# One chip program, re-ordered: an RWKV6 scan feeding a leaky-ReLU MLP, with the same steps in a new order and with other engine choices

## The chip, the cores and the metric

One core of a Trainium2 chip. Its engines are TensorE (PE: matmuls; PEld: its weight loads), VectorE (DVE), ScalarE (ACT), GpSimd (POOL) and SyncE (SP), which here issues nearly all DMAs. Each engine runs its own instructions in program order and waits on semaphores for the others. The metric is device time in microseconds of one execution, and the times given are medians over runs.

## The reference

Inputs r, k, v, w are (4 batches, 8 heads, 768 positions, 48), u is (8, 48). A recurrence with a 48 x 48 state for each head runs over the positions; its output, 3072 rows of 384, goes through a two-layer MLP (384 to 2048 to 384).

```python
for t in range(S):
    cur = einsum('bhd,bhe->bhde', u[None] * kt, vt)
    y[:, :, t] = einsum('bhd,bhde->bhe', rt, state + cur)
    state = wt[:, :, :, None] * state + einsum('bhd,bhe->bhde', kt, vt)
x = y.transpose(0, 2, 1, 3).reshape(B * S, H * D)
h = x @ w_in
g = maximum(0.01 * h, h)
out = g @ w_out
```

All is float32 outside; the kernel multiplies in bfloat16.

## The kernel before

**Tiling.** The positions are cut into 24 chunks of 128 (6 for each batch). Chunks 0 to 3 come as two pairs: the first 256 positions of batch 0 and of batch 1, loaded as 384 KB transfers. The other 20 chunks are singles with four loads of 192 KB each (w, k, r, v; L708), all on SyncE's queue. `seq` interleaves the batches, so that neighbouring chunks belong to different recurrences.

**One chunk** (`single`). ACT takes the logarithm of w (L718), PE sums it along the chunk with a triangular matrix (L724), DVE forms the other sum (`ci`, L736), ACT takes two exponentials (L750, L754), and DVE multiplies r and k by them (`rk`, through `mult`, L407). The transposes of r and k go through PE and an evacuation (L418; L423 on DVE or L425 on ACT) or, for the chunks in `RK_DMA` (among them 16 to 23), through a DMA transpose issued by SyncE (L771). PE makes the scores (L864), DVE masks them (two instructions, L795), PE multiplies the state (L831) and the masked scores (L836) with the inputs, and DVE adds the bonus term and writes y (L482). The bonus comes from POOL (L437, L441), a DVE reduction (L445) and POOL again (`vs`, L449). POOL also casts v (L457) and scales the state (L782). y is transposed into the columns of x by PE (L468) and a copy, or by a DMA transpose (L849; chunks 16, 17, 20 to 23).

**MLP.** The chunks are grouped into 14 blocks (`blocks`: 0 and 5 to 13 have two chunks, 1 to 4 one). A block's up products (L1030) fill a PSUM bank eight times (four times for one chunk), and ACT applies the leaky ReLU to each (L1045). The first seven blocks use plain down products (L1060) and one output copy for each chunk (L1071 on DVE, L1073 on ACT). The last seven (`seven`) use a seven-product scheme for 2 x 2 blocks of the down matrix: DVE forms four sums of the activations (L941) and, once, four of the weights (L910), PE makes the products (L960), and ACT and DVE combine them (L976, L974, L981). The weights come as float32 on the same SyncE queue: four loads of 384 KB and two of 768 KB of w_in (L318), four of 768 KB of w_out (L323); each is cast to bfloat16 by POOL, ACT or DVE (L340, L344, L342).

**The order.** Nothing is scheduled on the chip. The functions above only register steps with `Plan.add`: the engines that could do it, with an estimated duration each, what it depends on, and which tile slots it reads and takes. `Plan.order` then walks the list `ORDER` (1124 step numbers), gives each step its engine (`FORCE` where there is a choice), computes estimated start times from the durations, chooses for each buffer the slot that is free first by those times, and the instructions are emitted in that order. So `ORDER` fixes the instruction stream of each engine and the order of SyncE's queue, and a step that waits holds everything behind it on its engine. Ahead of the first up products the kernel fills PE's estimated gaps up to 24 us with matmuls on zeros (L1099).

The heart of it, shortened:

```python
for i in ORDER:
    e = FORCE.get(i) or next(iter(engs))
    now = max(at[e], ready[i])
    for b in takes:
        slot = min(free[b.pool])
    self.start[i], self.eng[i] = now, e
...
for i in order:
    plan.steps[i][1](plan.eng[i])
```

Of the kernel before, what the change touches and what calls it, by code (L numbers as in the profile page):

```python
# [22 lines left out]
class Plan:  # L23
# [4 lines left out]
    SEEN = {"PE": 0.21, "DVE": 0.05, "ACT": 0.05, "POOL": 0.07, "SP": 0.05}  # L28

# [3 lines left out]
    def add(self, engs, fn, pri, deps=(), reads=(), takes=(), wire=None):  # L33
        i = len(self.steps)
        self.steps.append([engs, fn, pri, {d for d in deps if d is not None}, tuple(reads), tuple(takes), wire])
        for b in (*reads, *takes):
            b.users.append(i)
        return i

    def order(self, pools):  # L40
# [11 lines left out]
        at, wire_free, landed, flying = dict(self.BEGIN), 0.0, 0.0, []  # L52
        for i in ORDER:
            engs, fn, deps, reads, takes, wire = self.steps[i][0], *self.steps[i][1:2], *self.steps[i][3:]
# [10 lines left out]
            for b in touched:  # L65
                if b.pool == "ps":
                    now = max([now, *(t for q, t in b.seen.items() if q != e)])
            self.start[i], self.eng[i] = now, e
# [24 lines left out]
LOAD = (1.1, 64, 1.4, 0.2)  # L93
BOTH = (1.5, 64, 1.45, 0.2)
WEIGHT = (2.08, 24, 2.6, 0.2)
HALF = (1.1, 16, 2.6, 0.2)
STORE = (0.45, 8, 0.9, 0.2)
TRK = (1.7, 64, 0.9, -0.6)
TY = (0.95, 24, 0.7, -0.6)
ORDER = [1122, 0, 1, 2, 3, 4, 5, 6, 7, 11, 14, 20, 12, 18, 15, 17, 16, 13, 19, 21, 8, 22, 25, 26, 27, 23, 36,  # L100
# [67 lines left out]
def kernel(  # L168
# [11 lines left out]
    nc = tc.nc  # L180
# [79 lines left out]
    with tc.manual_schedule():  # L260
# [193 lines left out]
        def cast_v(P0, slots, vv, vl):  # L454
            vb = Buf("vb")
            return vb, step(
                {"POOL": 0.56}, lambda e: nc.gpsimd.tensor_copy(out=vb.t[:], in_=vv()),  # L457
                P0 + 2, deps=vl, reads=slots, takes=[vb])
# [675 lines left out]
```

## Time and profile before

| | us |
|---|---|
| median of 3 runs | 179.06 |
| lowest and highest run | 178.73, 179.62 |
| profiled execution, first to last instruction | 177.0 |
| PE busy in it | 170.4 |
| DVE busy in it | 143.5 |
| ACT busy in it | 114.0 |
| POOL busy in it | 107.3 |

The profiled execution is one run of the program under the profiler. Its span counts from its first to its last instruction; the times of the runs also hold what lies around the program, and the page gives no figure for that. In the profile's lines, "L960 PE" is line 960 of the kernel on TensorE, `out<-in` names the tiles, "x48" is a count, and "idle before <-X" is time in which the engine stood still until X was done. "SPq" is SyncE's queue. The granted TensorE clock was 1.00 throughout.

### The profile page before, as it was taken

Reading aid. Unit: us, or ns where it says so; the run is one execution under the profiler, and the core shown is the slowest. Engines: PE = TensorE matmul, PEld = TensorE weight load, DVE = VectorE, ACT = ScalarE, POOL = GpSimd, SP = SyncE. Lnnn points to the kernel's source line nnn. Section 1 sums busy time; section 2 is a strip of 40 time slices with the busy share of each in tenths; the row PEclk is TensorE's granted clock in tenths of the full one; section 3 lists DMA queues with packets and bytes.
Section 4 is the critical chain, followed back from the end, with each engine's and each line's share of the span. In section 5 each row is a group of like instructions: output and inputs, shape, how many; then the busy total and the mean of one; then the engine's idle time right before and its main releaser. Section 6 shows DMA issues by size and latency. Waiting matters only on the chain.

```text
span 177.0 us, 5530 instructions
## 1 busy us (share of the span) xinstructions
PE 170.4 (96%) x2155; PEld 139.9 (79%) x2158; DVE 143.5 (81%) x299; ACT 114.0 (64%) x263; POOL 107.3 (61%) x143
## 2 busy tenths in 40 slices
PE   7999999999999999999999999999999998999993
PEld 2566779867768877777779899899899997799992
DVE  7498935267599899889879999999999999956662
ACT  5676769734677794796379964676769950178500
POOL 5989946486749859879599093391693959100000
PEclk9999999999999999999999999999999999999999
DMA  5999999999999999999999999996999897432104
GB/s 138 261 271 340 350 300 195 351 231 199 201 206 195 191 199 227 163 201 179 198 206 195 197 208 209 163 222 124 210 194 196 188 226 78 118 101 80 44 26 157
DMA packets 115885, 34.25 MB, mean 194 GB/s; under 512 B 108305, under 2 KB 115090, under 8 KB 115858
## 3 DMA queue, kind: packets, MB, share of 16 engines
q1 hardware_dynamic: 115856, 33.89, 93.1%
q8 instruction: 17, 0.28, 0.7%
q14 instruction: 10, 0.08, 0.2%
q10 hardware_dynamic: 2, 0.00, 0.0%
HBM read 25.17 MB, written 4.72 MB: 169 GB/s over the span
## 4 chain that ended last, share of the span: by engine, by line
PE 69%; DVE 15%; ACT 5%; issue 4%; DMA 3%; POOL 2%; DVEq 0%; SPq 0%; ACTq 0%
PE ps L1030 30%; PE ps L1060 13%; PE ps L960 10%; DVE rk L407 3%; DMA rkT<-rk 3%; PE ps L864 3%; DVE in L941 2%; PE ps L418 2%; ACT g L425 2%; PE ps L724 1%; PE ps L836 1%; DVE ci L736 1%; PE ps L518 1%; DVE dg L445 1%; ACT ps L750 1%
## 5 line engine op out<-in xcount | busy, mean ns | idle before, releaser
L1030 PE MATMUL ps<-xT,w_in_b 128*128 128x256 bf16 (+1 forms) x672 | 70.8, 258 | 0.3 <-DVE rk L407 0.2
L1045 ACT ACTIVATE g<-ps 128x512 bf16<-128x512 f32 x96 | 54.4, 598 | 18.1 <-PE ps L1030 16.0
L1030 PEld LDWEIGHTS <-w_in_b 128*128 128x128 bf16 x672 | 56.9, 98 | 7.8 <-issue 0.6
L437 POOL TENSOR_TENSOR ru<-in,ub 128x384 f32<-128x384 f32 x24 | 24.3, 1017 | 13.1 <-DMA in<-in_k_dram 7.0
L1060 PE MATMUL ps<-w_out_b,g 128*128 128x384 bf16 x160 | 31.4, 326 | 0.0
L407 DVE TENSOR_TENSOR rk<-in,ps 128x384 bf16<-128x384 f32 x48 | 24.8, 547 | 6.1 <-ACT ps L754 2.3
L782 POOL TENSOR_TENSOR sb<-s,a 128x384 bf16<-128x384 f32 x18 | 15.6, 875 | 16.6 <-ACT a L745 8.1
L795 DVE TENSOR_TENSOR m<-ps,maskb 128x512 bf16<-128x512 f32 x40 | 25.1, 682 | 0.3 <-PE ps L864 0.2
L441 POOL TENSOR_TENSOR ru<-ru,in 128x384 f32<-128x384 f32 x24 | 23.8, 1000 | 2.1 <-DMA in<-in_r_dram 1.1
L1060 PEld LDWEIGHTS <-g 128*128 128x128 bf16 x160 | 14.1, 97 | 6.8
L449 POOL TENSOR_TENSOR vs<-in,dg 128x384 f32<-128x384 f32 x20 | 17.4, 874 | 3.0 <-DMA in<-in_v_dram 2.1
L960 PEld LDWEIGHTS <-g 128*128 128x128 bf16 x224 | 18.3, 98 | 0.2
L976 ACT COPY o<-ps 128x192 f32<-128x192 f32 x18 | 5.8, 320 | 17.5 <-PE ps L960 15.5
L960 PEld LDWEIGHTS <-in 128*128 128x128 bf16 x168 | 13.6, 98 | 1.9 <-DVE in L941 1.4
L445 DVE TENSOR_REDUCE dg<-ru 128x8 f32<-128x384 f32 x24 | 12.9, 545 | 1.9 <-POOL ru L441 1.7
L457 POOL CAST vb<-in 128x384 bf16<-128x384 f32 x24 | 12.7, 534 | 2.2 <-DMA in<-in_v_dram 2.2
L981 DVE TENSOR_TENSOR o<-ps,o 128x192 f32<-128x192 f32 x35 | 11.6, 351 | 1.9 <-ACT o L976 1.1
L482 DVE TENSOR_TENSOR y<-ps,vs 128x384 bf16<-128x384 f32 x20 | 10.9, 553 | 2.4 <-PE ps L836 2.3
L754 ACT ACTIVATE ps<-ci 128x384 f32<-128x384 f32 x20 | 9.8, 493 | 4.7 <-DVE ci L736 4.1
L718 ACT ACTIVATE lw<-in 128x384 bf16<-128x384 f32 x20 | 9.9, 521 | 4.1 <-DMA in<-in_w_dram 4.1
L736 DVE TENSOR_TENSOR ci<-ps,lw 128x384 f32<-128x384 f32 x20 | 10.9, 551 | 1.8 <-PE ps L724 1.1
L960 PE MATMUL ps<-in,in 128*128 128x192 bf16 x112 | 11.4, 247 | 0.5 <-DVE in L941 0.5
(105 smaller groups left out, 258.8 us busy)
## 6 DMA issues: line engine op xcount, KB each, us to landing
out_dram<-o SPq DMA_DIRECT2D x23, 192.0 KB, 2.8
in<-in_w_dram SPq DMA_DIRECT2D x20, 192.0 KB, 4.7
in<-in_k_dram SPq DMA_DIRECT2D x20, 192.0 KB, 4.2
in<-in_r_dram SPq DMA_DIRECT2D x20, 192.0 KB, 4.2
in<-in_v_dram SPq DMA_DIRECT2D x20, 192.0 KB, 4.1
in<-in_moe_w_out_dram SPq DMA_DIRECT2D x4, 768.0 KB, 6.9
in<-in_moe_w_in_dram SPq DMA_DIRECT2D x2, 768.0 KB, 9.7
in<-in_moe_w_in_dram SPq DMA_DIRECT2D x4, 384.0 KB, 8.1
```

Of the source, the lines that this page charges most:

```text
L407: (nc.gpsimd if e == "POOL" else nc.vector).tensor_tensor(out=o, in0=x, in1=i, op=ALU.mult)
L437: lambda e: nc.gpsimd.tensor_tensor(out=ru.t[:], in0=kv(), in1=ubv, op=ALU.mult),
L441: lambda e: nc.gpsimd.tensor_tensor(out=ru.t[:], in0=ru.t[:], in1=rv(), op=ALU.mult),
L445: lambda e: nc.vector.tensor_reduce(out=dg.t[:], in_=ru.t[:], axis=AX.X, op=ALU.add),
L449: lambda e: nc.gpsimd.tensor_tensor(out=vs.t[:], in0=vv(), in1=dg.t[:].unsqueeze(2).to_broadcast([128, H, D]), op=ALU.mult),
L457: {"POOL": 0.56}, lambda e: nc.gpsimd.tensor_copy(out=vb.t[:], in_=vv()),
L782: lambda e: nc.gpsimd.tensor_tensor(out=sb.t[:].rearrange("p g a d -> p (g a) d"), in0=s_in.t[:].rearrange("p g a d -> p (g a) d"), in1=a_ ...
L795: lambda e, par=par: nc.vector.tensor_tensor(out=m.t[:, par, :, :], in0=sc[par].t[:].rearrange("p (g t) -> p g t", g=NP), in1=maskb[:].uns ...
L960: nc.tensor.matmul(o(), lhsT=x()[:, i, :], rhs=y()[:, i, :], start=fresh, stop=(stop and i == ii[-1]), skip_group_check=True)
L1030: nc.tensor.matmul(hp.t[:, a * N : (a + 1) * N], lhsT=w_in_b[:, t, (j + a) * 128 : (j + a + 1) * 128], rhs=xb.t[:, t, 0:N], start=(a == 0 ...
L1045: lambda e, hp=hp, g=g, j=j, J=J, N=N: nc.scalar.activation(out=g.t[:, j : j + J, 0:N], in_=hp.t[:, 0 : J * N].rearrange("p (a n) -> p a n ...
L1060: nc.tensor.matmul(op.t[:, 0:DM], lhsT=g.t[:, j, off : off + 128], rhs=w_out_b[:, j, :], start=(j == 0), stop=(j == NJ - 1))
```

## The change

No operation of the computation changes. Four things do:

1. `ORDER` and `FORCE` are new lists. 45 of the steps with a choice of engine change it: 20 leave DVE and 20 come to it, and the totals go from 281, 262 and 125 steps on DVE, ACT and POOL to 281, 265 and 122.
2. The planner's estimates change: the durations of some steps, the times of the DMA transfers, and three new terms: steps marked `alone` on DVE and POOL steps are kept apart in the estimate, a limit on outstanding DMA descriptors (`RING`), and DMA time taken by PE's instruction fetches (`mm`, `FETCHED`). They reach the chip only through the slot chosen for each buffer and through the number of warm-up matmuls.
3. The steps' priorities (`pri`) get small additions; the emitted order does not read them.
4. All PE steps that were registered before it depend on the step that takes the warm-up bank.

What the new `ORDER` does, told by the steps: the second pair's v is loaded ahead of all weights (it stood behind a 768 KB and a 384 KB piece of w_in); chunk 4's loads of w, k and r come ahead of the last 768 KB of w_in, and of all of w_out; chunk 6's r comes ahead of its k and of the last piece of w_out. At the end, chunk 23's w and k are loaded ahead of chunk 22's, DVE multiplies r and k of chunk 23 ahead of those of 22, the transposes (L771) go out as 20, 21, 23, 22 with the v of chunk 22 between 21 and 23 and the v of chunk 23 and a store between 23 and 22; DVE's four sums (L941) of block 11 stand behind the y (L482) of chunks 23 and 22, and four product steps of that block stand on PE among the up products of the last two blocks.

The diff, without the bodies of the two lists:

```diff
@@ Plan
+    RING, AFTER, FETCH = 145.0, 0.25, 1.0
+    FETCHED = [120, 235, *(128 * n + 65 for n in range(2, 17))]
-    def add(self, engs, fn, pri, deps=(), reads=(), takes=(), wire=None):
+    def add(self, engs, fn, pri, deps=(), reads=(), takes=(), wire=None, alone=False, mm=0):
@@ Plan.order
+            if e == "POOL" or alone and e == "DVE":
+                mine, other = (spans[e], spans["DVE" if e == "POOL" else "POOL"])
+                for a, z in other:
+                    if a <= now < z:
+                        now = z
...
-                while flying and sum(x for _, x in flying) + size > 150:
-                    at[e] = max(at[e], flying.pop(0)[0])
-                wire_free = max(wire_free, at[e] + lead) + time
-                flying.append((wire_free, size))
-                landed = self.done[i] = max(wire_free + lat, landed + 0.7 * time)
+                held = now
+                while flying and sum(x for _, x in flying) + size > self.RING:
+                    held = max(held, flying.pop(0)[0])
+                at[e] = max(at[e], held + self.AFTER)
...
+                flying.append((max(wire_free, *late), size))
+                self.done[i] = flying[-1][0] + lat
@@ transfer estimates
-LOAD = (1.1, 64, 1.4, 0.2)
+LOAD = (1.012, 64, 1.72, 0.45)
...
-TRK = (1.7, 64, 0.9, -0.6)
+TRK = (1.368, 64, 1.24, 0.7)
@@ the lists (start and end of ORDER)
-ORDER = [1122, 0, 1, 2, 3, 4, 5, 6, 7, 11, 14, 20, 12, 18, 15, 17, 16, 13, 19, 21, 8, 22, 25, 26, 27, 23, 36,
...
-    1115, 1116, 1112, 1113, 1119, 1117, 1118, 1121]
+ORDER = [0, 1, 4, 2, 1122, 3, 5, 6, 7, 11, 12, 14, 13, 8, 18, 22, 20, 25, 9, 23, 26, 19, 63, 21, 28, 29, 15, 36, 27,
...
+    1115, 1116, 1112, 1113, 1117, 1118, 1119, 1121]
-FORCE = {4: "ACT", 6: "DVE", 24: "ACT", 27: "ACT", 30: "DVE", 33: "ACT", 47: "ACT", 57: "ACT", 59: "DVE", 60:
...
+FORCE = {4: "DVE", 6: "DVE", 24: "DVE", 27: "ACT", 30: "ACT", 33: "ACT", 47: "DVE", 57: "ACT", 59: "ACT", 60: "ACT",
...
@@ durations, one for many
-                {"PE": 0.19 + 0.231 * len(ns)}, scores, ns[-1] * 10 + 1, deps=[s for x in asked for s in x[2]],
+                {"PE": 0.12 + 0.221 * len(ns)}, scores, ns[-1] * 10 + 1, mm=H * len(ns), deps=[s for x in asked for s in x[2]],
@@ warm-up
-        step({"PE": 0.0}, lambda e: None, 0.0, takes=[warm])
+        warm_from = step({"PE": 0.0}, lambda e: None, 0.0, takes=[warm])
+        for i in range(warm_from):
+            if "PE" in plan.steps[i][0]:
+                plan.steps[i][3].add(warm_from)
```

More of the change, by code (lines that the diff above doesn't have):

```diff
@@ L51, in order @@
         self.start, self.done, self.eng, ready = [None] * n, [0.0] * n, [None] * n, [0.0] * n
-        at, wire_free, landed, flying = dict(self.BEGIN), 0.0, 0.0, []
+        at, wire_free, flying = dict(self.BEGIN), 0.0, []
+        late, fetches, products, block = [0.0, 0.0], [], 0, 0
+        spans = {"POOL": [], "DVE": []}
         for i in ORDER:
-            engs, fn, deps, reads, takes, wire = self.steps[i][0], *self.steps[i][1:2], *self.steps[i][3:]
+            engs, fn, deps, reads, takes, wire, alone, mm = self.steps[i][0], *self.steps[i][1:2], *self.steps[i][3:]
             if left[i]:
@@ L67, in order @@
                     now = max([now, *(t for q, t in b.seen.items() if q != e)])
+            if e == "POOL" or alone and e == "DVE":
[3 more added lines that the diff above has]
+                        now = z
+                for a, z in other:
+                    if now < a < now + engs[e]:
+                        at["DVE" if e == "POOL" else "POOL"] += now + engs[e] - a
+                        break
+                mine.append((now, now + engs[e]))
+                del mine[:-3]
             self.start[i], self.eng[i] = now, e
@@ L345, in weight_steps @@
                 (win_s if which == 0 else wout_s).append(step(
-                    {"DVE": 0.57, "ACT": 0.83, "POOL": 0.86 if which == 0 else 0.96}, cast, pri + 1, deps=[ld], reads=[st]))
+                    {"DVE": 0.57, "ACT": 0.83, "POOL": 0.83}, cast, pri + 1, deps=[ld], reads=[st], alone=True))
         xt_steps, lns, firsts, rows = {}, {}, {}, {}
@@ L520, in go @@
                                 start=(j == 0 and x.start == 0), stop=(j == 1), skip_group_check=True)
-                return step({"PE": 0.33}, go, P0, deps=[s_ln], reads=[lw], takes=[bank])
+                return step({"PE": 0.33}, go, P0, mm=2 * (len(parts) if split else 1), deps=[s_ln], reads=[lw], takes=[bank])
             c1, c0, cg, e0 = (Buf("ps", "cp2") for _ in range(4))
@@ L636, in scores @@
                                     start=True, stop=True, skip_group_check=True)
-                s_sc = step({"PE": 0.42}, scores, P0 + 1, deps=s_T, reads=[rkT], takes=sc)
+                s_sc = step({"PE": 0.35}, scores, P0 + 1, mm=4 * NP, deps=s_T, reads=[rkT], takes=sc)
                 m = Buf("m")
@@ L730, in cum @@
                         rhs=ones[:], start=True, stop=True, skip_group_check=True)
-            s_cum = firsts[n] = step({"PE": 0.27}, cum, P0, deps=[s_ln], reads=[lw], takes=[cp])
+            s_cum = firsts[n] = step({"PE": 0.27}, cum, P0, mm=1 if first else 1 + NP, deps=[s_ln], reads=[lw], takes=[cp])
             ci, ek = Buf("ci"), Buf("ps", "ek")
@@ L809, in sums @@
                             start=True, stop=True, skip_group_check=True)
-                s_pp = step({"PE": 0.17}, sums, P0 + 2, deps=[s_k, s_vb, s_sb], reads=[rk, vb], takes=[pp])
+                s_pp = step({"PE": 0.17}, sums, P0 + 2, mm=NP, deps=[s_k, s_vb, s_sb], reads=[rk, vb], takes=[pp])
                 def state(e):
@@ L911, in mix @@
                 last = done[x] = step(
-                    {"DVE": 0.95}, sub, MIX_RANK, deps=[*wout_s, last], reads=t[: x // 2 + 1], takes=[t[x // 2]])
+                    {"DVE": 0.95}, sub, MIX_RANK, deps=[*wout_s, last], reads=t[: x // 2 + 1], takes=[t[x // 2]], alone=True)
             mixed.extend([part, t, done])
@@ L943, in seven @@
                     before = step(
-                        {"DVE": 0.68} if len(groups) == 1 else {"DVE": 0.42}, go, SUM_RANK + x * 0.5, deps=[*deps, before],
-                        reads=[g], takes=[sm])
+                        {"DVE": 0.69} if len(groups) == 1 else {"DVE": 0.42}, go, SUM_RANK + x * 0.5 + nb / 64, deps=[*deps, before],
+                        reads=[g], takes=[sm], alone=True)
                     s_sum.setdefault(name, []).append(before)
@@ L976, in go @@
                         nc.scalar.copy(out=o(), in_=x())
-                return step({"ACT": 0.33, "DVE": 0.35}, go, 3, deps=deps, reads=reads, takes=[to])
+                return step({"ACT": 0.33, "DVE": 0.35}, go, 3 + nb / 64, deps=deps, reads=reads, takes=[to])
             def plus(to, o, x, y, deps, reads):
@@ L1073, in ocopy @@
                         nc.scalar.copy(out=o.t[:], in_=op.t[:, 0:DM])
-                s_o = step({"DVE": 0.55, "ACT": 0.5}, ocopy, 3, deps=[s_dn], reads=[op], takes=[o])
+                s_o = step({"DVE": 0.55, "ACT": 0.5}, ocopy, 3 + ch / 64, deps=[s_dn], reads=[op], takes=[o])
                 step(
```

78 lines of the change are left out of this document (44 added, 34 removed), and 100 rows, old and new, of the table ORDER.

## The prediction

> **What bounds the kernel now.** I read the page first, then the busy time by stretches, then the chain of waits in order of time, and last single stretches engine by engine. The page's span, its row of engines and the chain's shares:
>
> ```profile
> span 177.0 us, 5530 instructions
> ...
> PE 170.4 (96%) x2155; PEld 139.9 (79%) x2158; DVE 143.5 (81%) x299; ACT 114.0 (64%) x263; POOL 107.3 (61%) x143
> ...
> PE 69%; DVE 15%; ACT 5%; issue 4%; DMA 3%; POOL 2%; DVEq 0%; SPq 0%; ACTq 0%
> ```
>
> The same execution in five stretches. The columns are the stretch, its length, busy us (and instructions) of PE, PEld, DVE, ACT, POOL, then clock, DMA share and GB/s:
>
> ```profile
> 0.00:25.00 25.00, 22.71 (x312) 14.44 (x316) 18.95 (x49) 16.59 (x34) 20.98 (x39) 1.00 1.06 277
> 25.00:55.00 30.00, 29.69 (x366) 22.75 (x364) 18.94 (x39) 20.87 (x46) 18.85 (x23) 1.00 1.11 231
> 55.00:145.00 90.00, 89.94 (x1147) 77.12 (x1145) 83.35 (x162) 65.46 (x162) 61.50 (x75) 1.00 1.05 195
> 145.00:155.00 10.00, 9.04 (x130) 7.80 (x128) 9.68 (x18) 1.03 (x3) 5.93 (x8) 1.00 0.65 105
> 155.00:177.00 22.00, 19.01 (x211) 17.81 (x208) 12.61 (x33) 10.01 (x20) 0.00 (x0) 1.00 0.25 82
> ```
>
> PE looks full, but that is the pipeline: a busy PE may still leave slots. The pace of matmuls that follow each other without a gap stands in the chain in order of time (start, us, what):
>
> ```profile
> 31.37 0.65 PE ps L1060 x4
> 32.02 0.67 PE ps L1030 x12
> ...
> 52.31 0.55 PE ps L864 x16
> ...
> 56.82 0.20 PE ps L836 x8
> ...
> 155.59 7.21 PE ps L1030 x66
> ...
> 166.09 7.93 PE ps L960 x96
> ```
>
> So a down product (L1060) takes 0.65/4 = 0.1625 us, an up product (L1030) 0.67/12 = 0.056 us at 128 columns and 7.21/66 = 0.109 at 256, a last-block product (L960) 7.93/96 = 0.0826, a score (L864) 0.034, a masked product (L836) 0.025. From 155.59 to 174.0 (166.09 + 7.93) PE runs at this pace: that part is its own and cannot be shortened by an order. The matmuls are the same in both kernels, so only PE's lost slots ahead of 155 us can be won or added to. I look for them in two stretches. First 145 to 155 us, all of PE's matmul groups (count, then busy us and mean ns):
>
> ```profile
> L960 PE MATMUL ps<-in,g 128*128 128x192 bf16 x32 | 3.1, 246 | 0.0
> L960 PE MATMUL ps<-in,in 128*128 128x192 bf16 x18 | 2.0, 248 | 0.5 <-DVE in L941 0.5
> L960 PE MATMUL ps<-w_out_b,in 128*128 128x192 bf16 x16 | 1.7, 248 | 0.4 <-DVE in L941 0.4
> L1030 PE MATMUL ps<-xT,w_in_b 128*128 128x256 bf16 x12 | 1.5, 272 | 0.0
> L836 PE MATMUL ps<-vb,m 128*128 128x48 bf16 x24 | 1.1, 184 | 0.0
> L831 PE MATMUL ps<-sb,rkT 128*128 128x96 bf16 x12 | 1.0, 206 | 0.0
> L864 PE MATMUL ps<-rkT 48*128 48x128 bf16 x16 | 0.8, 218 | 0.0
> ```
>
> 66 x 0.0826 + 12 x 0.109 + 24 x 0.025 + 16 x 0.034 = 7.9 us, and about 0.5 for the twelve L831 (between 12 x 0.025 and 12 x 0.056): 8.4 of 10 us. **About 1.6 us are lost here**, and DVE, 9.68 of 10 busy, is what PE waits for. Second, 40 to 50 us:
>
> ```profile
> L1060 PE MATMUL ps<-w_out_b,g 128*128 128x384 bf16 x30 | 5.9, 327 | 0.0
> L1030 PE MATMUL ps<-xT,w_in_b 128*128 128x128 bf16 x48 | 3.2, 219 | 0.2 <-DVE rk L407 0.2
> L418 PE MATMUL ps<-ident,rk 128*128 128x128 bf16 x8 | 0.8, 221 | 0.1
> L724 PE MATMUL ps<-lw,trev 128*128 128x384 bf16 x2 | 0.7, 326 | 0.0
> L836 PE MATMUL ps<-vb,m 128*128 128x48 bf16 x8 | 0.5, 184 | 0.0
> ```
>
> 30 x 0.1625 + 48 x 0.056 + 8 x 0.056 + 2 x 0.1625 + 8 x 0.025 = 8.5, and some 0.6 for the 19 short ones left out (0.025 to 0.056 each): 9.1. **About 0.9 us are lost.** From 55 to 145 us I treat the losses as what an order of this kind costs, and move nothing there.
>
> The Trainium skill, page Perfetto Trace Analysis, section Identifying the Most-Contended Engine, would have PE judged by the busy share of its weight loads; by that 37 us (177.0 - 139.9) would be free. The rows disagree: four L1060 take 0.65 us with four loads of about 0.1 us beside them, so 0.25 us of "free" load time is no free PE; the sum goes by the paces.
>
> **The change, part by part.** What runs is altered in three ways: the order of 1124 steps, the engine of 45 of them, and the count of warm-up matmuls (L1099), which fill gaps that the plan expects in the first 24 us. The planner's other new terms only choose tile slots and those gaps.
>
> *Engines.* 20 steps leave DVE and 20 come to it (281 before and after), ACT goes from 262 to 265, POOL from 125 to 122. The largest one-way group is five output copies that go from DVE to ACT:
>
> ```profile
> L1071 DVE COPY o<-ps 128x384 f32<-128x384 f32 x5 | 2.8, 550 | 0.0
> ```
>
> DVE loses those 2.8 us and two state copies (as long as these), and takes two weight casts, a state copy and a few smaller copies more: about 1 us less over 150 us. On its own I cost this at nothing, since PE sets the pace.
>
> *Start, 0 to 25 us.* The second pair's v is loaded ahead of all of w_in instead of after two pieces of it. POOL's row for the casts of that v:
>
> ```profile
> 19.36 0.96 POOL L457 CAST vb<-in 128x384 bf16<-128x384 f32 x2 [0.43 <-DMA in<-in_v_dram]
> ```
>
> Gain at most that 0.43 wait and about half a us of casts taken off POOL ahead of it, so -1.0; against it w_in comes one 384 KB load later while the first columns of x are ready at about the same time, which at worst holds the first up products for a load's time, +1.0. I take -0.2, near zero as both chains end within that us.
>
> *25 to 55 us.* The lost 0.9 follows on late inputs: DVE waits for chunk 6's r, and SyncE held that load long before it:
>
> ```profile
> 45.47 0.55 DVE L407 TENSOR_TENSOR rk<-in,ps 128x384 bf16<-128x384 f32 x1 [1.22 <-DMA in<-in_r_dram]
> ```
> ```profile
> 38.34 4.28 SPq L708 DMA_DIRECT2D in<-in_r_dram  x1
> ```
>
> In the new order chunk 6's r stands ahead of its k and of the last 768 KB piece of w_out; it stood behind both. The wait of 1.22 should go; the bounds are 0 (something else is late next: ACT's exponentials, or w_out, whose pieces come later) and -0.9. I take -0.6.
>
> *145 to 155 us.* DVE's rows for the four sums (L941) of block 11 (chunks 18 and 19), 142.7 to 151.6:
>
> ```profile
> 142.72 0.68 DVE L941 TENSOR_TENSOR in<-g 128x1024 bf16<-128x1024 bf16 x1
> 143.44 0.69 DVE L941 TENSOR_TENSOR g<-g 128x1024 bf16<-128x1024 bf16 x1
> ...
> 149.02 1.30 DVE L941 TENSOR_TENSOR in<-in,g 128x1024 bf16<-128x1024 bf16 x1
> ...
> 150.51 1.04 DVE L941 TENSOR_TENSOR in<-g,in 128x1024 bf16<-128x1024 bf16 x1
> ```
>
> Two are stretched (1.30 and 1.04 against 0.68) while POOL works:
>
> ```profile
> 148.94 2.07 POOL L449 TENSOR_TENSOR vs<-in,dg 128x384 f32<-128x384 f32 x2
> ```
>
> The new order puts all four, and two additions (0.35 each), behind chunk 22's y (L482), after which POOL has nothing left to collide with. That takes 0.68 + 0.69 + 1.30 + 1.04 + 0.7 = 4.4 us from ahead of that y, less 0.55 for chunk 23's y, now ahead of it: 3.8. Where PE and DVE met before:
>
> ```profile
> 153.38 0.34 PE L831 MATMUL ps<-sb,rkT 128*128 128x96 bf16 x4
> ```
> ```profile
> 154.14 0.54 DVE L482 TENSOR_TENSOR y<-ps,vs 128x384 bf16<-128x384 f32 x1
> ```
>
> DVE could be at that y by 154.1 - 3.8 = 150.3. On PE, four product steps (32 x 0.0826 = 2.6 us) now stand behind chunk 22's L831 and chunk 23's (0.4) ahead, so without lost slots PE comes to it at 153.4 - 1.6 - 2.6 + 0.4 = 149.6. So the end moves by the new time of that L831, less 153.4, plus 2.2: at 149.6 all 1.6 us are won. DVE allows it, as its masks stand 2 us ahead of the y. What is late next is the transpose that feeds them. The two last transposes by SyncE, chunk 22's and then chunk 23's, and the page's row for all of them (KB, then median us to landing):
>
> ```profile
> 142.50 2.20 SPq L771 DMA_TRANSPOSE rkT<-rk  x1
> ...
> 147.51 1.24 SPq L771 DMA_TRANSPOSE rkT<-rk  x1
> ```
> ```profile
> rkT<-rk SPq DMA_TRANSPOSE x13, 3.8
> ```
>
> Their order is swapped: chunk 22's is now the last. DVE's r and k for both come earlier (chunk 23's pass three sums, four masks and chunk 22's pair), so I expect it near 143.5, landed at 147.3, with scores and two masks (0.4 + 1.4) L831 near 149.5 to 150.5. I take 150.0, a gain of 1.2; bounds -1.6 and +1.8 (rival B).
>
> *Tail.* The last four product steps and additions are unchanged: 0.
>
> Sum: -0.2 - 0.6 - 1.2 = -2.0, so a span of 175.0. The runs shown have a median of 179.06, 2.06 above the profiled span of 177.0, and I carry that over: **177.1 us**.
>
> A rule that speaks against: the Trainium skill, SBUF — State Buffer, section Who interferes with whom, lets casts on DVE as well as sums with two SBUF inputs lock out POOL for a whole instruction, or be locked out. The stretched sums above agree. The change puts three weight casts on DVE where one was, while POOL is 20.98 of 25 us busy; no DVE cast beside POOL work is in this trace. By that rule up to two POOL instructions of about 1 us more would be blocked early, which lies inside the +1.0 of the start.
>
> **Rivals.** *A, no change:* the DMA queue sets the end of the scan. Its share is 1.05 to 1.11 from 25 to 145 us, so the last chunks' r and k can't land much earlier, whatever their order; chunk 22's transpose, now behind chunk 23's, is issued near 144.5, and L831 comes at 151.0: -0.2 there. With -0.2 from the earlier parts: 178.7.
>
> *B, slower:* SyncE serves its queue in order, and chunk 22's transpose stands behind chunk 23's, chunk 23's v and a store. If chunk 23's r or k is late on DVE, all of these are held, and the second place in the queue stays where it is, at 147.5: landed at 151.3, scores and masks to 153.1, L831 hardly earlier than now, and 2.6 us of products still to be done behind it. The end moves by +1.8, less 0.8 from the earlier parts: 180.1. It decides from L831 at 152.0 on, 1.4 us ahead of now. Against it: the diff puts chunk 23's r and k early on DVE, and its loads ahead of chunk 22's.
>
> *C, more:* all 1.6 and 0.9 are won, the start gives 0.7, and 1 us of small losses between 55 and 145 us goes too, the stretched sums from 137 us on among them: -4.2, 174.9.
>
> **Chances.** Forecast (175.7 to 178.1) 0.56, C 0.10, A 0.19, B 0.15. This measurement can tell about 0.5% (0.9 us) from no change: faster 0.66, same 0.19, slower 0.15. The range 175.0 to 179.8 leaves out most of B and half of C, 2 in 10.
>
> **What would show it.** Right: chunk 22's L831 at 150 or before, sums of that block at 0.68 with POOL idle, the first up product no later than before, no wait for chunk 6's r. Wrong: PE short of work before chunk 22's L831, the last transpose issued after 145, or the first up product over 1 us later than before. If PE loses new slots between 55 and 145 us, my zero there is the failed step.

## The result and the profile after

| | before | after |
|---|---|---|
| median of 5 runs, us | 179.06 | 184.57 |
| lowest and highest run | 178.73, 179.62 | 184.07, 185.1 |
| span of the profiled execution | 177.0 | 182.4 |

The ratio is 1.0292, 95% interval 1.0254 to 1.0330: the kernel is 5.5 us slower, where 177.1 us and at most 179.8 were predicted. In all that follows, medians and ranges are those of runs in the chip's fast state. The page of after, its span, its engines and the shares of the chain that ended last:

```profile
span 182.4 us, 5481 instructions
...
PE 169.2 (93%) x2153; PEld 139.3 (76%) x2156; DVE 143.7 (79%) x299; ACT 114.7 (63%) x266; POOL 108.2 (59%) x140
...
PE 26%; DMA 19%; DVE 14%; POOL 13%; SPq 11%; issue 9%; ACT 5%; DVEq 0%; POOLq 0%
```

The engines do nearly the same work as before (VectorE 143.7 us against 143.5, GpSimd 108.2 against 107.3). What changed is who ends the waits: PE's share of the chain falls from 69% to 26%, and transfers and SyncE's queue (DMA, SPq), 3% before, have 30%. The stretches of the prediction, now for after (stretch, its length, busy us and instructions of PE, PEld, DVE, ACT, POOL, clock, DMA share, GB/s):

```profile
0.00:25.00 25.00, 20.96 (x312) 13.40 (x316) 20.19 (x51) 17.80 (x37) 18.89 (x37) 1.00 1.05 249
25.00:55.00 30.00, 29.73 (x381) 23.42 (x380) 17.03 (x34) 21.79 (x47) 16.40 (x21) 1.00 1.16 241
55.00:145.00 90.00, 85.77 (x1069) 72.19 (x1066) 80.53 (x155) 62.19 (x155) 65.07 (x74) 1.00 1.09 191
145.00:155.00 10.00, 9.73 (x149) 8.70 (x147) 9.96 (x20) 3.25 (x9) 7.88 (x11) 1.00 0.69 154
155.00:182.40 27.40, 23.01 (x254) 21.58 (x251) 15.96 (x41) 9.64 (x20) 0.00 (x0) 0.98 0.22 74
```

Before, PE was busy 89.94 of the 90 us from 55 to 145; now it is 85.77, with 1069 matmuls where 1147 were done. Up to 55 us after does more matmuls (312 + 381 against 312 + 366). So the loss lies between 55 and 145 us. To place it finer I take the time less the useful matmul time begun by then, each matmul counted at its pace in the prediction (0.02 to 0.06 us for the short ones; 156.5 us in all, the same in both kernels). What is left is the time that PE has lost so far. The level of a row hangs on the paces taken for shapes that the prediction did not time; the differences between two kernels hardly do:

```
us from the start     25     55     70     85    115    145    160    170
before, lost       12.53  14.00  14.30  14.62  15.25  15.49  17.36  17.34
after, lost        12.37  13.38  13.59  15.75  18.12  20.10  21.97  21.96
after less before  -0.16  -0.62  -0.71  +1.13  +2.87  +4.61  +4.61  +4.62
```

After is 0.7 us ahead at 70 us, loses 5.3 us against before from there to 145, and nothing behind it. Single profiles scatter by some 0.6 us: two kernels below whose first 90 us are those of before and of after (light_before and light_after) differ by +0.4 us at 25 us, -0.1 at 55, -0.2 at 70 and +4.4 at 145. So the lead up to 70 us is within the scatter, and the loss behind it is far outside. The rest of the 5.4 us of span is in the tail. Both kernels issue five last stores there (SyncE's rows in order of time, before and then after: start, us, what):

```profile
169.21 5.55 SPq L1013 DMA_DIRECT2D out_dram<-o  x5
```
```profile
174.06 5.34 SPq L1035 DMA_DIRECT2D out_dram<-o  x5
```

The last one is issued by 174.76 us in before and by 179.40 in after, 4.6 us apart; from there to the end before takes 2.2 us and after 3.0. What the 0.75 us more are spent on is not shown.

GpSimd's longest waits for loads in after and, below them, the two of before that they answer to (who waits for whom: us in total, times, longest):

```profile
POOL ru L458 <- DMA in<-in_k_dram: 10.4, 6, 4.5
POOL vb L478 <- DMA in<-in_v_dram: 9.2, 5, 3.6
```
```profile
POOL ru L437 <- DMA in<-in_k_dram: 7.0, 3, 3.3
...
POOL vb L457 <- DMA in<-in_v_dram: 2.2, 4, 0.9
```

These are 19.6 us for k and v in after and 9.2 in before over the whole span. But 7.4 of after's 9.2 us for v lie ahead of 55 us, where after loses nothing against before. GpSimd's waits for loads from 55 to 145 us alone, after and then before:

```profile
POOL ru L458 <- DMA in<-in_k_dram: 10.1, 5, 4.5
...
POOL ru L462 <- DMA in<-in_r_dram: 2.8, 2, 1.7
...
POOL vb L478 <- DMA in<-in_v_dram: 1.8, 1, 1.8
...
POOL vb L478 <- DMA in<-in_k_dram: 1.3, 1, 1.3
```
```profile
POOL ru L437 <- DMA in<-in_k_dram: 3.7, 2, 2.9
...
POOL vs L449 <- DMA in<-in_v_dram: 2.1, 1, 2.1
...
POOL vb L457 <- DMA in<-in_v_dram: 0.9, 1, 0.9
...
POOL ru L441 <- DMA in<-in_r_dram: 0.3, 1, 0.3
```

That is 16.0 us in after and 7.0 in before. The first of these waits that reaches PE can be followed row by row. SyncE issues chunk 10's k as the first of the two k at 66.65 us, behind its r and v and two loads of w for chunks 13 and 12; GpSimd stands for it until 71.94, VectorE's product of k (third row) until 71.96, and PE's transposes of that product leave a gap until 72.57. The row of its weight loads (PEld), which bring that product in, names VectorE; PE's own names ScalarE's copy of an earlier transpose, which ended at 72.53. So these rows alone do not tell which of the two held PE; but in a_edf below, where this k is loaded earlier, PE loses 0.1 us from 70 to 75 us where after loses 1.5:

```profile
62.85 0.73 SPq L729 DMA_DIRECT2D in<-in_r_dram  x1
63.62 0.95 SPq L729 DMA_DIRECT2D in<-in_v_dram  x1
64.62 1.99 SPq L729 DMA_DIRECT2D in<-in_w_dram  x2
66.65 3.18 SPq L729 DMA_DIRECT2D in<-in_k_dram  x2
```
```profile
71.94 1.00 POOL L458 TENSOR_TENSOR ru<-in,ub 128x384 f32<-128x384 f32 x1 [4.55 <-DMA in<-in_k_dram]
```
```profile
71.96 1.48 DVE L428 TENSOR_TENSOR rk<-in,ps 128x384 bf16<-128x384 f32 x3 [1.69 <-DMA in<-in_k_dram]
```
```profile
72.57 0.40 PE L439 MATMUL ps<-ident,rk 128*128 128x128 bf16 x4 [0.90 <-ACT rkT L446]
```
```profile
72.57 0.23 PEld L439 LDWEIGHTS <-rk 128*128 128x128 bf16 x4 [1.18 <-DVE rk L428]
```

The DMA queue is full in both kernels up to 145 us (shares 1.05 to 1.16), so there is no idle stretch in which a late load could be made up. In bytes, after has moved 249 x 25 + 241 x 30 = 13.46 MB by 55 us, before 13.86; by 145 us 30.65 against 31.41. It is two loads' worth behind at 55 us and four at 145, while its PE is ahead at 55.

### The profile page after: what moved, and what is told of

Same layout as the page of the kernel before. It is cut to its first block, busy times and chain, and to the rows that moved or that the text cites. A ratio compares the mean times of both kernels' runs of the same rounds, so it can differ in the third digit from the quotient of the medians.

```text
span 182.4 us, 5481 instructions
## 1 busy us (share of the span) xinstructions
PE 169.2 (93%) x2153; PEld 139.3 (76%) x2156; DVE 143.7 (79%) x299; ACT 114.7 (63%) x266; POOL 108.2 (59%) x140
## 4 chain that ended last, share of the span: by engine, by line
PE 26%; DMA 19%; DVE 14%; POOL 13%; SPq 11%; issue 9%; ACT 5%; DVEq 0%; POOLq 0%
PE ps L1052 12%; PE ps L981 8%; DMA rkT<-rk 6%; SPq L515 5%; DMA in<-in_k_dram 5%; DMA in<-in_moe_w_in_dram 4%; POOL vs L470 3%; DVE m L816 3%; SPq L729 3%; ACT g L1067 3%; POOL ru L458 3%; POOL sb L803 3%; DVE in L962 3%; DVE rk L428 3%; DMA in<-in_r_dram 2%
## 5 line engine op out<-in xcount | busy, mean ns | idle before, releaser
L1052 PE MATMUL ps<-xT,w_in_b 128*128 128x256 bf16 (+1 forms) x672 | 72.2, 257 | 1.3 <-DMA xT<-y 0.6
L1067 ACT ACTIVATE g<-ps 128x512 bf16<-128x512 f32 x96 | 54.4, 600 | 19.9 <-PE ps L1052 19.6
L1052 PEld LDWEIGHTS <-w_in_b 128*128 128x128 bf16 x672 | 55.6, 98 | 7.8 <-DMA xT<-y 0.7
L458 POOL TENSOR_TENSOR ru<-in,ub 128x384 f32<-128x384 f32 x24 | 24.6, 1032 | 10.6 <-DMA in<-in_k_dram 10.4
L1082 PE MATMUL ps<-w_out_b,g 128*128 128x384 bf16 x160 | 30.8, 326 | 0.0
L470 POOL TENSOR_TENSOR vs<-in,dg 128x384 f32<-128x384 f32 x20 | 18.0, 906 | 6.6 <-DVE dg L466 6.6
L1082 PEld LDWEIGHTS <-g 128*128 128x128 bf16 x160 | 14.3, 97 | 7.1
L803 POOL TENSOR_TENSOR sb<-s,a 128x384 bf16<-128x384 f32 x18 | 17.4, 968 | 2.7 <-ACT a L766 2.7
L981 PEld LDWEIGHTS <-g 128*128 128x128 bf16 x224 | 18.7, 98 | 0.4
L998 ACT COPY o<-ps 128x192 f32<-128x192 f32 x16 | 5.1, 319 | 13.2 <-PE ps L981 13.2
```

Source lines behind the costliest of these rows:

```text
L458: lambda e: nc.gpsimd.tensor_tensor(out=ru.t[:], in0=kv(), in1=ubv, op=ALU.mult),
L470: lambda e: nc.gpsimd.tensor_tensor(out=vs.t[:], in0=vv(), in1=dg.t[:].unsqueeze(2).to_broadcast([128, H, D]), op=ALU.mult),
L803: lambda e: nc.gpsimd.tensor_tensor(out=sb.t[:].rearrange("p g a d -> p (g a) d"), in0=s_in.t[:].rearrange("p g a d -> p (g a) d"), in1=a_ ...
L981: nc.tensor.matmul(o(), lhsT=x()[:, i, :], rhs=y()[:, i, :], start=fresh, stop=(stop and i == ii[-1]), skip_group_check=True)
L1052: nc.tensor.matmul(hp.t[:, a * N : (a + 1) * N], lhsT=w_in_b[:, t, (j + a) * 128 : (j + a + 1) * 128], rhs=xb.t[:, t, 0:N], start=(a == 0 ...
L1067: lambda e, hp=hp, g=g, j=j, J=J, N=N: nc.scalar.activation(out=g.t[:, j : j + J, 0:N], in_=hp.t[:, 0 : J * N].rearrange("p (a n) -> p a n ...
```

## The experiments

Theory **T1**: the engines of after stand on loads that the full queue brings too late. **T2**: engine choices, DVE and GpSimd in each other's way. **T3**: the order of the late part. Later **T6**: VectorE has no slack, and what it comes late with it stays late with; **T8**: the lag of the stream in the first 60 us is the cause.

### 1536-byte loads, half sums, and both

The first edit, in the loads of the single chunks:

```diff
-in_=src[b, :, t0 : t0 + L, :].rearrange("h p d -> p h d")
+in_=src[b].rearrange("h (x r) d -> (h x) (r d)", r=8)[c * L : c * L + L].rearrange("p (h d) -> p h d", h=H)
```

> The kernel after, in which the 72 loads of the single chunks read the same number of bytes from their tensors as 128 rows of 1536 bytes instead of 1024 rows of 192 (so what lands is not the chunk's own layout; every step, wait and engine is as in after). Theory T1 (the new order needs its loads sooner than the saturated DMA stream brings them, and the engines stand on late k, v and r): most of the 5.5 us comes back, 174 to 178 us, and below the same edit of before. Rival T2 (engine choices: DVE and GpSimd in each other's way): stays 182 to 185. Rival T3 (the order of the late part itself): stays above 181.

> The same edit in the kernel before: the loads of the single chunks as 1536-byte rows. T1: the old order hardly waits for loads after 55 us, so little is won, 176.5 to 179 us, and the order of the two kernels turns round (after-with-fast-loads is the faster). T2 and T3: before stays some 5 us the faster of the two.

The second edit, in the sums and in the products that read them:

```diff
-out=o()[:, i0:i1], in0=in0()[:, i0:i1], in1=in1()[:, i0:i1], op=op)
+out=o()[:, i0:(i0 + i1) // 2], in0=in0()[:, i0:(i0 + i1) // 2], in1=in1()[:, i0:(i0 + i1) // 2], op=op)
-o(), lhsT=x()[:, i, :], rhs=y()[:, i, :],
+o(), lhsT=x()[:, i // 4 * 4 + i % 2 if own else i % 4, :], rhs=y()[:, i, :],
```

> The kernel after, in which each of the 32 instructions of the sums (L962) adds only half of its columns, and the products read the half that was made twice (so the products' values are wrong; all steps, waits, engines and matmuls stay). It takes about 0.3 us from VectorE some 28 times between 95 and 155 us and leaves the loads as they are. Theory T6 (VectorE has no idle time left from 100 us on, so what it comes late with at 100 us it stays late with): most of what after loses from 100 to 160 us comes back, 180 to 182 us; what is lost before 95 us stays. T1 alone (late loads everywhere): 183.5 to 184.6 us.

> The same edit in the kernel before. T6: little room, since its matmuls lose only some 2.5 us after 100 us: 177 to 179 us, and the gap to after-with-light-sums falls from 5.5 us to 2 to 4. T1 alone: the gap stays at 5 to 5.5.

> The kernel after with both edits, the 1536-byte loads and the half sums. T6 and T1 together: both losses go, 176 to 178 us. If VectorE is not what holds the late part, the 180.4 us of the fast loads alone stay.

> The kernel before with both edits, the 1536-byte loads and the half sums, the partner of the 177.9 us of after with both. If late loads and a VectorE without slack are the whole of it, the two come out within 1 us of each other, 176.5 to 177.5 us for this one; if something else in the new order costs as well, before stays ahead by more: 174.5 to 176 us.

Measured, medians in us; the ratios to before of the same chip and their intervals stand below the table:

| | as it is | 1536-byte loads | half sums | both |
|---|---|---|---|---|
| order of before | 179.06 | 177.23 | 178.50 | 176.41 |
| order of after | 184.57 | 180.39 | 183.57 | 177.90 |
| after less before | 5.5 | 3.2 | 5.1 | 1.5 |

After with 1536-byte loads is 1.0085 (1.0056 to 1.0115), before with them 0.9916 (0.9887 to 0.9945); with half sums 1.0216 (1.0149 to 1.0283) and 0.9954 (0.9923 to 0.9985); with both 0.9937 (0.9909 to 0.9964) and 0.9839 (0.9787 to 0.9891).

The first edit is in all 80 loads of the 20 singles (the first expectation says 72). Faster loads take 4.2 us from after and 1.7 from before, so 2.3 of the 5.5 us go. T1's own numbers (174 to 178 for after, and below before) are missed, and so are those of T2 (182 to 185) and T3 (above 181): loads are the largest part, not the whole. The edit unloads the whole queue, so "late loads" here takes in the transposes and weights on it. Half sums alone give after 1.0 us, within the intervals nothing sure: T6 alone falls. But on top of fast loads they give 2.5 us. In after's order VectorE lies right behind the loads. From 115 to 145 us, first after with fast loads alone, then after with both, last before with fast loads alone:

```profile
115.00:145.00 30.00, 29.38 (x376) 26.90 (x374) 29.61 (x59) 19.91 (x53) 22.92 (x25) 1.00 0.68 173
```
```profile
115.00:145.00 30.00, 30.00 (x394) 27.65 (x392) 28.16 (x62) 21.30 (x56) 21.20 (x26) 1.00 0.71 183
```
```profile
115.00:145.00 30.00, 30.00 (x397) 27.68 (x395) 29.36 (x59) 21.36 (x55) 19.57 (x25) 1.00 0.72 178
```

VectorE was 29.61 of 30 us busy and PE was not; with VectorE at 28.16, PE is full. A full VectorE does not do this by itself: in the order of before it is 29.36 us busy and PE is full all the same. Shorter sums also leave VectorE and GpSimd less time in each other's way (T2), and no run separates that from T6. The last 1.5 us (1.8 by the ratios, as the two kernels with both edits ran on different chips) are in neither. In their two profiles 0.8 us of it lie ahead of 25 us, where profiles scatter by about as much, and 0.6 between 110 and 115.

### Only some of the loads made fast

```diff
+if n in (4, 5):        # after_fast45; after_fast10: n >= 10
+    at = src[b].rearrange("h (x r) d -> (h x) (r d)", r=8)[c * L : c * L + L].rearrange("p (h d) -> p h d", h=H)
```

> The kernel after, in which only the eight loads of chunks 4 and 5 (issued from 18 to 42 us) read 1536-byte rows; it gives the queue some 3 us back before 45 us, more than the 2 us by which its stream is behind that of before at 60 us. T8 with its cause in the first 60 us: 180 to 181.5 us, and the loss from 70 to 110 us is gone. If the new order behind 60 us is slow whatever the loads before it did: 183 to 184.6 us.

> The kernel after, in which only the loads of chunks 10 to 23 (issued from 56 us on) read 1536-byte rows; the first 56 us are as in after. All loads so gave 4.2 us back, those of chunks 4 and 5 alone 2.0. If each stretch loses for itself by its own late loads: about 2 us back, 182 to 183 us. If the lag laid down before 56 us is what the late loads come from: 183.5 to 184.6 us. If the late loads behind 56 us are all that matters: 180.4 to 181 us.

The first gave 182.61 us (182.18 to 182.99), 2.0 back, between its two cases, the second 181.04 (180.43 to 182.82; ratio 1.0103, 1.0058 to 1.0149), 3.5 back, at the edge of its last case. Together they would be 5.5, all loads gave 4.2. So the early lag counts, but the loads behind 56 us cost more and cost by themselves: with chunks 4 and 5 made fast PE has lost only 13.16 us at 75 us (before: 14.48), and then 7.1 us more by 160, before 2.9. T8 in the form "the first 60 us are the cause" falls.

### The loads in the order of their use

The edit permutes 51 of the list's entries, all of them loads of single chunks; around chunk 10:

```diff
-w11, v8, w10, v9, r11, r10, v10, w13, w12, k10, k11
+w10, v8, v9, w11, k10, r10, r11, w13, w12, k11, v10
```

> The kernel after, with only the order of the single chunks' loads on SyncE changed: the same 80 places, but in each the load whose first user comes next in the kernel's order (51 entries of the order move, most by one to five places; for example chunk 10's k ahead of chunk 13's and 12's w, chunk 14's k and r ahead of chunk 17's, chunk 19's v ahead of chunk 20's and 23's). No engine's own order or work changes. Theory T1a (after stands on loads because loads wanted later are queued ahead of loads wanted now): GpSimd's waits for k and v fall from 19.6 us by half, and 2 to 4 us come back, 180.5 to 182.5 us. Rival T1b (the stream as a whole is too late, and no order of loads within it helps): 184 to 185 us, the waits only change names.

It ran 184.4 us (182.52 to 184.83), as after does. The waits of GpSimd, now:

```profile
POOL vb L475 <- DMA in<-in_v_dram: 15.2, 9, 4.2
...
POOL ru L455 <- DMA in<-in_k_dram: 3.1, 2, 2.1
```

The wait for k went from 10.4 to 3.1 us and that for v from 9.2 to 15.2: 18.3 in all where 19.6 were (from 55 to 145 us, 11.1 where 11.9 were). The lost time moved as well: 1.7 us more than in after by 55 us, 1.7 less from there to 145. T1a falls, T1b stands: this re-sorting found no load whose place was the trouble, and what one stretch wins another loses.

### Old and new order put together

Four mixes take one kernel's steps (and their engines) up to a time of its own plan and the rest in the other's order:

```diff
+early = [i for i in ORDER_BEFORE if start[i] < 110]        # b60_a: 60, b140_a: 140
+ORDER = early + [i for i in ORDER_AFTER if i not in early]   # a50_b: the two lists exchanged, 50
```

> The new order and engines for the 306 steps that the new plan starts before 50 us, and from there the old order and engines for what is left; slots and warm-ups by the new planner's constants. T1 (the loss is made from 70 us on, by the order that follows there): 176.5 to 179 us. A rival T5 (the loss is laid down at the start, by loads put out of order in the first 50 us and by the new constants): 182 to 185.

> The old order and engines for what the old plan starts before 110 us, and the new order and engines for what is left. T1: about half of the lost time is lost before 110 us in the kernel after, and here isn't: 179 to 182 us. T3 (the late part of the new order is what is slow): 183 to 186. T5 (start): 178 to 180.

> The old order and engines for what the old plan starts before 60 us, the new ones behind it. The stream of loads is then in time at 60 us. If what is lost in after is lost through its stream of the first 60 us: 179 to 181 us. If the new order behind 60 us loses it by itself: 182.5 to 185 us.

> The old order up to 110 us and the new one behind it, with the 1536-byte loads. Without them this mix lost 3.3 us against before, all of it behind 115 us. If that is late loads: 177 to 178.5 us, as before-with-fast-loads (177.2). If it is the new order of VectorE's late work: 179.5 to 181 us.

| | us | lowest, highest | ratio to before, interval |
|---|---|---|---|
| a50_b: new to 50 us, then old | 180.87 | 180.81, 181.62 | 1.0117, 1.0080 to 1.0155 |
| b60_a: old to 60 us, then new | 184.28 | 183.48, 185.94 | 1.0328, 1.0266 to 1.0389 |
| b110_a: old to 110 us, then new | 182.26 | 182.09, 182.73 | 1.0189, 1.0154 to 1.0225 |
| fast_b110_a: the same, 1536-byte loads | 178.58 | 177.34, 179.22 | 0.9946, 0.9908 to 0.9983 |

a50_b falls between the numbers of T1 and of its rival, b110_a just above T1's, b60_a in its second case, fast_b110_a just above its first. The old order behind a new start loses 2.4 us at the seam, the place where the one order passes into the other (14.2 to 16.6 from 55 to 70 us, before 0.3), and then nothing more than before does: PE's lost time goes from 17.1 at 95 us to 17.9 at 145, before from 14.75 to 15.5.

```profile
75.00:145.00 70.00, 69.94 (x888) 60.71 (x886) 64.57 (x129) 50.89 (x128) 45.96 (x57) 1.00 1.02 191
```

The new order behind an old start loses all the same: 16.3 at 60 us to 22.0 at 140 in b60_a (5.7 us, before 1.5), 15.2 at 110 to 20.8 at 160 in b110_a (5.6 us, before 2.4). So the start of after is not what loses it; the order behind 60 us is. Nor are the new planner's slots and warm-ups, which a50_b has too. (The profile of b60_a is its slowest run, with PE at half its clock from 43 to 46 us, in the old part; its runs at a granted clock of 1.00 took 183.48 and 183.82.) Fast loads take 3.7 us from b110_a and 1.7 from before, which leaves it 1.35 behind before with fast loads (177.23), or 0.5 by the ratios, as the two ran on different chips: there too most is late loads. One limit: the seam itself costs, as a50_b shows, so these sizes are not those of the same stretches in after.

### The two steps that the forecast priced, each alone in the old order

```diff
-203, ..., 173, 142, 144, 143, 188, 189, 204, 216, 218, 743, 223, 227, 205, 215
+203, ..., 173, 205, 142, 144, 143, 188, 189, 204, 216, 218, 743, 223, 227, 215
```

(205 is chunk 6's r, 204 its k, 142 the last piece of w_out.)

> The kernel before with one entry of its order moved: chunk 6's r is loaded ahead of its k and of the last 768 KB piece of w_out instead of behind both, the step that the forecast gave 0.6 us (with 0 and 0.9 as its ends). If the forecast's step holds: 178.1 to 178.7 us, and no wait of VectorE for that r. If the piece of w_out or k is late instead: 179 us or above.

> The kernel before with the new order only for what the old plan starts behind 140 us (about 160 steps, the four sums of block 11 behind chunk 22's y among them): the forecast's late step alone, which it gave 1.2 us, with its slower rival at +1.8. If the forecast's step holds: 177.4 to 178.4 us. If the loads and transposes in their new order come too late here too: 179.5 to 181 us.

> Both at once: the kernel before with chunk 6's r moved and the new order behind 140 us. If both steps hold they add up, 177 to 178 us, and this beats both kernels. If only one does, it shows that one's time.

before_r6 took 179.17 us beside 178.92 for before (ratio 1.0009, 0.9993 to 1.0026): no gain. The wait for that r is gone, but what is late next is k. The forecast's lower end, 0, had allowed for something else being late next, though it named ScalarE's exponentials and w_out:

```profile
45.21 1.02 DVE L400 TENSOR_TENSOR rk<-in,ps 128x384 bf16<-128x384 f32 x2 [1.25 <-DMA in<-in_k_dram]
```

b140_a took 182.94 (1.0220, 1.0195 to 1.0245), 4.0 us more than before, and both together 183.08 (1.0241, 1.0218 to 1.0264). In b140_a, from the chain of waits, then from VectorE's, ScalarE's and PE's rows:

```profile
138.99 4.25 DMA in<-in_r_dram
```
```profile
143.36 1.16 DVE L400 TENSOR_TENSOR rk<-in,ps 128x384 bf16<-128x384 f32 x2 [1.02 <-ACT ps L747]
144.43 1.88 DVE L788 TENSOR_TENSOR m<-ps,maskb 128x512 bf16<-128x512 f32 x3
```
```profile
143.95 0.17 ACT L738 ACTIVATE a<-ps 64x4 f32<-64x4 f32 x1 [0.70 <-DVE rk L400]
```
```profile
144.17 1.48 PE L953 MATMUL ps<-in,g 128*128 128x192 bf16 x16 [1.90 <-ACT a L738]
...
155.13 1.05 PE L1023 MATMUL ps<-xT,w_in_b 128*128 128x256 bf16 x8 [1.50 <-DMA xT<-y]
```

Chunk 23's r and k stand ahead on VectorE, as the forecast wanted them, but the r lands at 138.99 + 4.25 = 143.24, and ScalarE's exponential for the product, which VectorE's row names, was done at that time too, at 143.25. ScalarE's `a` (the factors that scale the state) stands behind that product, and PE stands for it for 1.90 us at 144. The masks of the chunks before stand behind it as well (144.43), and PE stands for 1.50 more at 155, where the transposes of y come late.

### Lateness put into the kernel before

```diff
-nc.vector.tensor_tensor(out=ci.t[:], ...)
+for _ in range(6 if n == 10 else 1):                              # before_6ci
+    nc.vector.tensor_tensor(out=ci.t[:], ...)
-nc.sync.dma_start(out=part(i)(), ...)
+for _ in range(2 if (n, i) in ((4, 2), (5, 0)) else 1):           # before_2ld
+    nc.sync.dma_start(out=part(i)(), ...)
```

> The kernel before, in which VectorE does chunk 10's one addition of ci six times instead of once (the same result each time): 5 x 0.55 = 2.75 us more VectorE work at 67 us, and nothing else. T6: from there VectorE has no slack, so nearly all of it is on the end: 181 to 182.3 us. Rival (VectorE has slack as its 81 % of the span says): it is made up, 179 to 180 us.

> The kernel before, in which two loads (chunk 4's r and chunk 5's w, at 24 to 25 us) are done twice, the second time with the same rows: 2 x 192 KB more on the queue, which is about 2 us of its time, and nothing else. Theory T8 (the queue is full from 5 to 145 us, so every load behind is late by as much, and nothing behind has slack for it): 181 to 183.5 us. Rival (the loads behind have slack, and order and engines set the time): 179 to 180 us.

before_6ci: 182.64 us (180.81 to 182.69; ratio 1.0149, 1.0069 to 1.0228), its profiled span 179.1, 2.1 above before's. The six additions:

```profile
66.19 3.50 DVE L736 TENSOR_TENSOR ci<-ps,lw 128x384 f32<-128x384 f32 x6
```

PE's lost time is 1.7 us above before's at 70 us and 2.0 at 160: of 2.75 us of VectorE work at 67 us about three quarters are paid in the profiled execution, and nothing is won back. The median shows more than the whole of it, but the profiled run (180.81 us) had a granted clock of 0.999 and the others 0.989 to 0.991, so part of that surplus may be the clock's. T6 holds in this: the 19% of the span in which VectorE is idle are little slack at that place.

before_2ld: 185.3 us (183.99 to 186.42), 6.6 above before, more than T8 has. The edit did more than intended. SyncE took 5.66 us over the two r, as it held the second back for 4.8 us (it writes the same place as the first, which is the likely reason). The queue ran low, with a DMA share of 0.74 from 25 to 40 us where before has 1.15; the weights behind came late, and PE stood for them:

```profile
24.28 5.66 SPq L709 DMA_DIRECT2D in<-in_r_dram  x2
```
```profile
39.80 1.59 POOL L340 CAST w_out_b<-in 128x768 bf16<-128x768 f32 x2 [6.09 <-DMA in<-in_moe_w_out_dram]
```
```profile
41.44 5.28 PE L1061 MATMUL ps<-w_out_b,g 128*128 128x384 bf16 x16 [3.05 <-POOL w_out_b L340]
```
```profile
40.00:48.00 8.00, 6.56 (x36) 3.67 (x36) 1.37 (x3) 0.52 (x1) 6.28 (x8) 0.57 0.98 222
```

All of its loss lies between 35 and 50 us (lost time 12.6 to 20.8); from 55 to 145 us it loses 1.6 us, as before does. So the run settles nothing on T8, but shows that the old order carries a uniform lateness through that stretch without growing it.

## Why the prediction was wrong

**Start, -0.2.** Measured -0.16 at 25 us, but +0.4 in light_after against light_before, whose start is the same. The term is small, as forecast; its sign is within the scatter, and that the number fits is luck.

**25 to 55 us, -0.6.** Measured a further -0.46 (-0.56 in light_after against light_before), so the size was right. The reason given, chunk 6's r alone, was not: by itself it gives 0, so the fit is luck or another part of the new order.

**55 to 145 us: "I treat the losses as what an order of this kind costs, and move nothing there."** This is the step that failed: the cost of the new order there was put at nothing, and the prediction's last line had named that zero as the step to doubt. Measured +5.2 us (from -0.62 to +4.61), nearly the whole result. The prediction had read PE 89.94 of 90 us busy and the DMA share of 1.05 in one row, and VectorE's 83.35, and priced single moves against PE's lost slots alone. But three resources were full there at once: the queue, with no idle stretch in which a late load is made up; PE; and VectorE, by this row of before, to 28.96 of 30 us:

```profile
115.00:145.00 30.00, 30.00 (x395) 27.57 (x393) 28.96 (x58) 22.66 (x59) 19.51 (x24) 1.00 1.00 195
```

The old order loses 1.5 us there, as its engines mostly find their next input in place. A list of 1124 steps rewritten there has no cost of zero by default: it has to be shown that its inputs come as it asks for them, load by load, and here they did not (16.0 us of GpSimd's waits for k, r and v in this stretch against 7.0).

**145 to 155 us, -1.2.** Measured 0 (+4.61 at 145 and at 160 us). Chunk 22's products with the state, expected at 150.0, are the first row of after, and the first up product of block 12 the second:

```profile
154.94 0.33 PE L852 MATMUL ps<-sb,rkT 128*128 128x96 bf16 x4
...
156.11 1.16 PE L1052 MATMUL ps<-xT,w_in_b 128*128 128x256 bf16 x9 [0.63 <-DMA xT<-y]
```

The kernel was 4.6 us late by then, which explains most of 154.94; the step's gain is not there either way. Its transpose, expected near 143.5, is the second of these and was issued at 148.0, behind chunk 23's transpose, chunk 23's v and a store:

```profile
145.39 1.24 SPq L792 DMA_TRANSPOSE rkT<-rk  x1
146.72 0.53 SPq L729 DMA_DIRECT2D in<-in_v_dram  x1
147.30 0.61 SPq L1035 DMA_DIRECT2D out_dram<-o  x1
148.01 1.26 SPq L792 DMA_TRANSPOSE rkT<-rk  x1
```

This is the queue of rival B, which had been priced at +1.8; alone in the old order the late part costs 4.0, and how much of that is the seam's is not shown.

**Tail, 0.** Measured +0.75, behind the same five stores; the cause is open. The terms add up: -0.16 - 0.46 + 5.23 + 0 + 0.75 = 5.4, the difference of the spans.

**Rivals and chances.** Rival A named the resource, the queue, but took it as a reason for no change: a full queue that brings the same loads in another order is no neutral bound. The chance of 0.15 for slower rested on one place at the end and left out that the 90 us in the middle could lose.

**What the runs settle.** The order behind 60 us loses it, late loads are the largest part (2.3 of 5.5 us against before, 4.2 in all), and VectorE without slack the next (1.7, once the loads are fast). Loads before 45 us count too: those of chunks 4 and 5 made fast gave 2.0 us back. The engine choices were not tried alone, so what they cost (T2) stays open. The total work of VectorE and GpSimd is nearly unchanged, and VectorE's sums are 1.0 us longer in total. What stays open are the last 1.5 us, and why this order asks for its loads earlier than they come. With the same loads, none of the orders tried is faster than that of before.

## What to carry to other kernels

Where the DMA queue, VectorE and PE are all full in a stretch, price a new order there as a loss until the landing times show that each engine finds its next input. In both trials here a wait that went when loads were moved came back at another load: longer rows for the loads gave time in both orders (4.2 and 1.7 us), less VectorE work gave more on top of that, and moving loads gave none. Cut a tuned list of steps in two only with care, as the seam of a50_b cost about 2 us.

## What the runs showed of the hardware

**Short rows load the queue more.** With the same bytes in 1536-byte rows the DMA share from 55 to 145 us fell from 1.05 to 0.68 in the order of before, at 188 GB/s against 195:

```profile
55.00:145.00 90.00, 89.96 (x1141) 77.24 (x1139) 84.10 (x162) 64.82 (x161) 62.92 (x75) 1.00 0.68 188
```

The Trainium skill, page DMA: Bandwidth & Descriptors, section Specifications, gives 512 bytes as the smallest transfer for full rate; the runs agree, as with the 192-byte rows the queue's share for about the same bytes was 1.5 times as high.

**A starved PE can come back at half its clock.** In before_2ld the 16 down products from 41.44 us took 5.28 us, 0.33 each, where 0.1625 is the pace, and the granted clock from 40 to 48 us is 0.57. So 16 x 0.1675 = 2.7 us of that run's loss are the clock's, not the load's. The Trainium skill, page TensorE: Matmul & The Clock Gate, Part 1, has the array fall to half rate after at least one idle window of some 3.4 us and return after at least one of sustained work. The rows agree in kind, not to the microsecond: PE had stood for 3.05 us, and the granted clock was still 0.50 from 46 to 47 us, 5 us after the work began again. In b60_a a standstill of 2.06 us, up to 41.76, was followed by a granted clock of 0.81 from 40 to 45 us and 0.85 from 45 to 50. In after the waits are short, and the clock is 1.00 in every stretch up to 155 us.
